# Sixteen tiny loads in the load queue of a retention and two-MLP kernel's prologue

## The chip, the cores and the metric

The kernel runs on one core of a Trainium2 chip, in one launch. The time is the device time of that core in microseconds, as the median of several runs. Beside the runs there is one profiled execution, from which all rows below come.

## What is computed

Retention over q, k and v (4 batches, 8 heads, 576 tokens, 64 dimensions), then two MLPs over the 2,304 tokens of 512 features, each with 2,048 hidden features, all in float32:

```
scores = (q @ k.T) / 8
D[i, j] = gamma[h] ** (i - j)  where i >= j, else 0;  gamma[h] = 1 - 2 ** (-5 - h)
x  = (scores * D) @ v                     # heads side by side: 2304 x 512
h  = max(x @ w_in, 0);  x = (h * h) @ w_out
h  = x @ w2_in;  y = (h * clip(h + 3, 0, 6) / 6) @ w2_out
```

## The kernel before

The tokens stand in 18 chunks of 128. The first MLP goes over five blocks of 512 or 384 tokens and, within a block, over 16 slices `f` of 128 hidden features: `h_part` (line 645) makes h of a slice, `a_part` (line 689) adds its part of the output to four accumulators. The retention of the first four chunks is done in a prologue (the functions named `first_...`), that of the others in between the slices of the first MLP (`retention`, `visit`). The second MLP follows with other tiles (lines 1243 and 1298).

Matrix products on TensorE take each float32 operand as two parts, a rounded one and its residue. The weights of the first MLP come as 64-bit words, so each half slice, a tile of 512 KB (128 rows of 4 KB), goes through four steps: `load_w` brings it (line 133; tile `raw_0_f_i`, half i of slice f: i = 0 is for h, i = 1 for the accumulation), `scale_w` scales its two halves on ScalarE (lines 143, 144), `narrow_w` joins them on VectorE (lines 161, 162), `cast_w` rounds on ScalarE (line 170) and `low_w` makes the residue on GpSimd or VectorE (line 177). The order of the instructions on each engine is the order in which the code is written.

The prologue's loads are all issued on SyncE, in one order, written out by hand. The tiles that they fill: `q_c` holds q and k of chunk c transposed (line 211, 512 KB), `kv_c` k and v by rows (line 217, 512 KB), `con0` and `con` three pieces of the constants (lines 887, 891, 904); `con` is the last of them, first read by `scale_k` of chunk 4 (line 419).

```python
    load_t(0)
    nc.sync.dma_start(con0[:, :QD0], cst[:, :QD0])
    load_kv(0)
    load_t(1)
    load_kv(1)
    nc.sync.dma_start(con0[:, QD0:], cst[:, QD0:DK0])
    load_t(2)
    load_kv(2)
    load_w(0, 0, (0,))
    load_t(3)
    load_kv(3)
    load_w(0, 1, (0,))
    ...
    load_w(0, 3, (1,))
    nc.sync.dma_start(con, cst[:, DK0:])
```

Behind them SyncE issues, for chunk 4, `k`, `q`, `v` and four pieces of `qs` (lines 225, 226, 233, 412), and then the weights from slice 4 on. Every load raises one of eight semaphores, DMAHW0 to DMAHW7, which are given to the loads in turn; before SyncE issues a load, it waits until the load that had the same semaphore before has landed, that is the one eight places ahead. SyncE goes through its instructions in order, so a load that waits holds up all behind it.

The compute part of the prologue ends with `h_part(0, 0, 0)`, whose tokens come in two halves; the second half needs `x` of chunk 3 (`first_x(3)`, line 338, on ScalarE). On ScalarE the order there is: cast w_0_0_0, scale raw_0_1_0, x of chunk 3, scale raw_0_0_1, cast w_0_1_0 (made from raw_0_1_0 and read by the second `h_part`), scale raw_0_2_0.

`align` is a tile of 128 x 80 float32 that only takes room: nothing reads or writes it.

Of the kernel before, what the change touches and what calls it, by code (L numbers as in the profile page):

```python
# [11 lines left out]
F32 = mybir.dt.float32  # L12
# [7 lines left out]
P = 128  # L20
# [69 lines left out]
def retention_moe_kernel(ctx: ExitStack, tc, qk, kv, w1, w2, cst, out):  # L90
# [5 lines left out]
    nc = tc.nc  # L96
# [3 lines left out]
    def pool(stack, name, bufs, **kw):  # L100
        return stack.enter_context(tc.tile_pool(name=name, bufs=bufs, reuse_waits="tile", **kw))

    left, right = ExitStack(), ExitStack()
# [4 lines left out]
    xapool = pool(left, "xapool", 1, side="left")  # L108
    whi = pool(left, "whi", 1, side="left")

    pool(ctx, "align", 1, side="right").tile([P, 80], F32, tag="align", name="align")
    upool = pool(ctx, "upool", 1, side="right")
    wlo = pool(right, "wlo", 1, side="right")
    xbpool = pool(right, "xbpool", 1, side="right")
# [13 lines left out]
    def load_w(ph, f, halves=(0, 1)):  # L128

        src = w1.bitcast(I32)  # L130
        for i in halves:
            t = (wlo if f < NJ else whi).tile([P, DM, 2], I32, tag=f"w{f}_{i}", name=f"raw_{ph}_{f}_{i}")
            nc.sync.dma_start(
                t, src[f, :, 2 * DM * i : 2 * DM * (i + 1)].rearrange("p (n t) -> p n t", t=2)
            )
            raws[ph, f, i] = t
# [68 lines left out]
    def load_t(c):  # L205
        if c:
            tag = (None, f"w{NF - 5}_0", f"w{NF - 2}_0", f"w{NF - 2}_1")[c]
            t = whi.tile([P, 2, NPAIR, P], F32, tag=tag, name=f"q_{c}")
        else:
            t = apool.tile([P, 2, NPAIR, P], F32, tag="q", name=f"q_{c}")  # L210
        nc.sync.dma_start(t, qk[c].rearrange("p x (n t) -> p x n t", n=NPAIR))
        ch[c] = [t[:, 0], t[:, 1]]

    def load_kv(c):
        tag = (f"w{NF - 6}_0", f"w{NF - 5}_1", f"w{NF - 3}_0", f"w{NF - 3}_1")[c]
        t = whi.tile([P, 2, DM], F32, tag=tag, name=f"kv_{c}")
        nc.sync.dma_start(t, kv[c])
        ch[c] += [t[:, 0], t[:, 1]]
# [506 lines left out]
    def new_x(ph, blk):  # L725
        nb, tag = BLOCKS[blk]
        p = xbpool if tag == "xb" else xapool
        xs[ph, blk] = p.tile([P, 2, NC, nb], F32R, tag=tag, name=f"x_{ph}_{blk}")
# [142 lines left out]
            fn(*a)  # L871


    nc.gpsimd.memset(nought, 0.0)

    def idle_matmuls(n):
# [17 lines left out]
    load_w(0, 0, (0,))  # L894
    load_t(3)
    load_kv(3)
    load_w(0, 1, (0,))
    load_w(0, 0, (1,))
    load_w(0, 2, (0,))
# [1 line left out]
    load_w(0, 3, (0,))  # L901
    load_w(0, 2, (1,))
    load_w(0, 3, (1,))
    nc.sync.dma_start(con, cst[:, DK0:])
    new_x(0, 0)

# [446 lines left out]
```

## Time and profile before

| | us |
|---|---|
| median of 3 runs | 801.71 |
| lowest and highest | 801.16, 802.65 |
| the profiled execution, its own time | 802.4 |
| its span, first to last instruction | 800.6 |
| TensorE busy | 794.1 |
| VectorE, ScalarE, GpSimd busy | 587.1, 400.9, 165.3 |

In the profile PE is TensorE's matmuls, PEld its weight loads, DVE VectorE, ACT ScalarE, POOL GpSimd, SP SyncE; L133 is line 133 of the kernel. Names of tiles have their numbers left out, so that raw stands for every raw_0_f_i. Times count from the first instruction. A load's time to landing runs from the start of its issue on SyncE until its last part is in place.

### The profile page before, as it was taken

How to read it: one execution, taken by the hardware profiler on the slowest of the kernel's cores; microseconds unless marked ns; L12 is line 12 of the kernel's file. 1: busy time of each engine (PE TensorE's matmuls, PEld its weight loads, DVE VectorE, ACT ScalarE, POOL GpSimd, SP SyncE). 2: the span in 40 equal slices, each digit the busy share in tenths (PEclk: the TensorE clock that was granted, in tenths of full speed). 3: DMA queues.
4: the chain of work that ended last, by engine and by line, in shares of the span. 5: the costliest groups of instructions: out<-in, count | busy, mean ns of one | idle time of the engine just before them, and what ended most of it. 6: DMA issues, size and time to landing. Idle time of an engine off the chain costs nothing.

```text
span 800.6 us, 16540 instructions
## 1 busy us (share of the span) xinstructions
PE 794.1 (99%) x6396; PEld 740.2 (92%) x6396; DVE 587.1 (73%) x1083; ACT 400.9 (50%) x746; POOL 165.3 (21%) x154
## 2 busy tenths in 40 slices
PE   8999999999999999999999999999999999999998
PEld 7878889999888899998888899999999999999998
DVE  4888987888755577775547876988577987677864
ACT  4797745444444444444445533666234655244553
POOL 4212230211001011100000065600255500256300
PEclk9999999999999999999999999999999999999999
DMA  9966627777746487856448887988887979877884
GB/s 340 344 222 222 221 93 221 221 221 229 217 139 199 123 249 222 224 159 191 138 141 263 246 303 253 321 294 292 276 260 247 355 255 305 277 242 260 272 278 142
DMA packets 148062, 189.66 MB, mean 237 GB/s; under 512 B 22416, under 2 KB 101904, under 8 KB 147984
## 3 DMA queue, kind: packets, MB, share of 16 engines
q1 hardware_dynamic: 147984, 188.61, 73.8%
q8 instruction: 50, 0.82, 0.4%
q14 instruction: 28, 0.23, 0.1%
HBM read 149.78 MB, written 38.80 MB: 236 GB/s over the span
## 4 chain that ended last, share of the span: by engine, by line
PE 95%; ACT 2%; DVE 1%; DMA 1%; issue 0%; POOL 0%; SPq 0%; DVEq 0%; ACTq 0%; POOLq 0%
PE acc L689 24%; PE h L645 23%; PE z L1243 22%; PE z L1298 21%; PE at L518 2%; DMA kv<-kv_dram 1%; PE alone L518 0%; PE o L282 0%; ACT w L170 0%; ACT raw L143 0%; ACT raw L144 0%; DVE wt L162 0%; PE sums L282 0%; PE sc L261 0%; DVE r L663 0%
## 5 line engine op out<-in xcount | busy, mean ns | idle before, releaser
L689 PE MATMUL acc<-g,w 128*128 128x512 f32 (+1 forms) x960 | 212.6, 370 | 0.0
L645 PE MATMUL h<-x,w 128*128 128x512 f32 (+2 forms) x972 | 211.1, 365 | 0.3 <-ACT w L170 0.3
L645 PEld LDWEIGHTS h<-x,w 128*128 128x128 f32 x972 | 175.8, 188 | 23.2 <-ACT w L170 0.7
L689 PEld LDWEIGHTS acc<-g,w 128*128 128x128 f32 x960 | 173.8, 188 | 23.7 <-DVE g L671 0.3
L1243 PE MATMUL z<-xop,ring 128*128 128x384 f32 x1008 | 175.3, 334 | 0.0
L1243 PEld LDWEIGHTS z<-xop,ring 128*128 128x128 f32 x1008 | 174.7, 188 | 0.1
L1298 PE MATMUL z<-ring,spl 128*128 128x256 f32 x1512 | 172.2, 276 | 0.0
L1298 PEld LDWEIGHTS z<-ring,spl 128*128 128x128 f32 x1512 | 172.1, 188 | 0.0
L1159 POOL TENSOR_TENSOR aop<-aop,aop 128x384 f32<-128x384 f32 x96 | 108.1, 1137 | 293.4 <-DVE aop L1156 289.6
L1181 DVE TENSOR_TENSOR spl<-aop,spl 128x384 fp32r<-128x384 f32 x168 | 98.5, 604 | 31.2 <-ACT spl L1177 29.2
L1177 ACT ACTIVATE spl<-aop 128x384 fp32r<-128x384 f32 x168 | 86.3, 523 | 54.5 <-PE z L1298 48.5
L660 ACT ACTIVATE r<-h 128x512 f32<-128x512 f32 (+1 forms) x79 | 43.7, 553 | 110.8 <-PE h L645 110.7
L1153 ACT ACTIVATE aop<-held,small 128x384 f32<-128x384 f32 x72 | 44.4, 617 | 108.4 <-DVE held L1119 107.9
L663 DVE TENSOR_TENSOR r<-r,h 128x512 f32<-128x512 f32 (+1 forms) x80 | 50.6, 632 | 52.2 <-ACT r L660 51.4
L1119 DVE TENSOR_TENSOR held<-z,held 128x384 f32<-128x384 f32 x120 | 66.5, 554 | 28.6 <-PE z L1243 26.5
L665 ACT ACTIVATE g<-r 128x512 fp32r<-128x512 f32 (+1 forms) x80 | 47.1, 589 | 64.2 <-DVE r L663 64.2
L671 DVE TENSOR_TENSOR g<-r,g 128x512 fp32r<-128x512 f32 (+1 forms) x80 | 53.8, 672 | 20.9 <-ACT g L665 18.5
L1156 DVE SCALAR_TENSOR_TENSOR aop<-aop,held 128x384 f32<-128x384 f32 x72 | 50.1, 696 | 17.8 <-ACT aop L1153 16.1
L415 POOL TENSOR_TENSOR qs<-qs,con 128x512 f32<-128x512 f32 x11 | 14.9, 1359 | 138.0 <-DMA qs<-qk_dram 125.7
L779 ACT ACTIVATE uhi<-seven 128x896 fp32r<-128x896 f32 x32 | 30.5, 955 | 24.1 <-DVE seven L769 13.7
L784 DVE TENSOR_TENSOR seven<-seven,uhi 128x896 fp32r<-128x896 f32 x32 | 34.9, 1091 | 7.8 <-ACT uhi L779 7.5
L177 POOL TENSOR_TENSOR w<-wt,w 128x512 fp32r<-128x512 f32 x14 | 19.0, 1357 | 69.2 <-ACT w L170 59.8
(114 smaller groups left out, 610.0 us busy)
## 6 DMA issues: line engine op xcount, KB each, us to landing
ring<-w_out_hl SPq DMA_DIRECT2D x84, 512.0 KB, 4.9
ring<-w_in_hl SPq DMA_DIRECT2D x72, 512.0 KB, 4.8
raw<-w_dram SPq DMA_DIRECT2D x32, 512.0 KB, 7.0
uraw<-w_dram SPq DMA_DIRECT2D x64, 256.0 KB, 3.3
q<-qk_dram SPq DMA_DIRECT2D x18, 512.0 KB, 5.4
w_in_hl<-uhi SPq DMA_DIRECT2D x16, 448.0 KB, 3.7
w_in_hl<-seven SPq DMA_DIRECT2D x16, 448.0 KB, 4.5
w_out_hl<-uhi SPq DMA_DIRECT2D x16, 448.0 KB, 3.3
```

Source lines behind the costliest of these rows:

```text
L645: nc.tensor.matmul(hp[:, ts], w[:, wi, c * P : (c + 1) * P], x[:, xi, c, ts], start=k == 0, stop=k == 3 * NC - 1,)
L663: nc.vector.tensor_tensor(r, r, hp[:, :nb], ALU.mult)
L665: nc.scalar.activation(g[:, 0, :nb], r, AF.Copy)
L671: nc.vector.tensor_tensor(g[:, 1, :nb], r, g[:, 0, :nb].bitcast(F32), ALU.subtract)
L689: nc.tensor.matmul(acc[d][:, :nb], wt, g[:, gi, :nb], start=first, stop=stop)
L1119: fn(*a)
L1156: stt(f32(q, j), f32(q, j), 6.0, h, ALU.min, ALU.mult)
L1159: nc.gpsimd.tensor_tensor(f32(o, j), f32(a, j), f32(b, j), op)
L1177: act(t[:, 0, :], f32(q, k), AF.Copy)
L1181: tt(t[:, 1, :], f32(q, k), t[:, 0, :].bitcast(F32), ALU.subtract)
L1243: nc.tensor.matmul(bank[q], w[:, wi, u * P : (u + 1) * P], x[:, u, xi, :], start=k == 0 and q not in (2, 4, 3), stop=k == 5, skip_group_ch ...
L1298: nc.tensor.matmul(o, sp[:, g, P * n : P * (n + 1)], w[:, k % 2, wi, :], start=k == 0 and m == 0 and n % 2 == 0 and q not in (2, 4, 3), st ...
```

## The change

The tile that only took room gets a name, and two sets of eight loads write into it: 2, 4, 6, 8, 10, 12, 14 and 15 rows of 5 to 12 numbers (20 to 48 bytes) of the table of constants, side by side. The first set stands behind the load of kv_3, the second ahead of the load of `con`. Nothing reads what they bring. Lines behind the new function move by 6 to 8.

```diff
-    pool(ctx, "align", 1, side="right").tile([P, 80], F32, tag="align", name="align")
+    spare = pool(ctx, "align", 1, side="right").tile([P, 80], F32, tag="align", name="align")
...
+    def small_loads():
+        at = 0
+        for i, n in enumerate((2, 4, 6, 8, 10, 12, 14, 15)):
+            nc.sync.dma_start(spare[:n, at : at + 5 + i], cst[:n, :5 + i])
+            at += 5 + i
+
...
     load_t(3)
     load_kv(3)
+    small_loads()
     load_w(0, 1, (0,))
...
     load_w(0, 2, (1,))
     load_w(0, 3, (1,))
+    small_loads()
     nc.sync.dma_start(con, cst[:, DK0:])
     new_x(0, 0)
```

The first place is on SyncE, at the load of kv_3, in the kernel before. In brackets stands the semaphore that the instruction waits for (the number behind its name has no meaning here); align is the spare tile, w1_dram the first MLP's weights.

```order
L211 DMA q_3_147<-qk_dram 128x1024 [waits DMAHW1_49]
L217 DMA kv_3_149<-kv_dram 128x1024 [waits DMAHW2_49]
L133 DMA raw_0_1_0_151<-w1_dram 128x1024 [waits DMAHW3_49]
L133 DMA raw_0_0_1_153<-w1_dram 128x1024 [waits DMAHW4_49]
L133 DMA raw_0_2_0_155<-w1_dram 128x1024 [waits DMAHW5_49]
L133 DMA raw_0_1_1_157<-w1_dram 128x1024 [waits DMAHW6_49]
```

The same place in the changed kernel:

```order
L217 DMA kv_3_149<-kv_dram 128x1024 [waits DMAHW2_49]
L877 DMA align_73<-cst_dram 2x5 [waits DMAHW3_49]
L877 DMA align_73<-cst_dram 4x6 [waits DMAHW4_49]
L877 DMA align_73<-cst_dram 6x7 [waits DMAHW5_49]
L877 DMA align_73<-cst_dram 8x8 [waits DMAHW6_49]
L877 DMA align_73<-cst_dram 10x9 [waits DMAHW7_49]
L877 DMA align_73<-cst_dram 12x10 [waits DMAHW0_49]
L877 DMA align_73<-cst_dram 14x11 [waits DMAHW1_49]
L877 DMA align_73<-cst_dram 15x12 [waits DMAHW2_49]
L133 DMA raw_0_1_0_159<-w1_dram 128x1024 [waits DMAHW3_49]
```

The eight new loads take each of the eight semaphores once; the last of them, align with 15 rows, has the semaphore of kv_3 and waits for kv_3 to land. Raw_0_1_0 stands behind it and waits for the first of the new loads, where it waited for q_1, which stood eight places ahead.

The second place is on SyncE, at the load of con, in the kernel before (k_4 is the next chunk's k):

```order
L133 DMA raw_0_2_1_161<-w1_dram 128x1024 [waits DMAHW0_49]
L133 DMA raw_0_3_1_163<-w1_dram 128x1024 [waits DMAHW1_49]
L904 DMA con_102<-cst_dram 128x1040 [waits DMAHW2_49]
L225 DMA k_4_400<-kv_dram 128x512 [waits DMAHW3_49]
```

and in the changed kernel:

```order
L133 DMA raw_0_3_1_171<-w1_dram 128x1024 [waits DMAHW1_49]
L877 DMA align_73<-cst_dram 2x5 [waits DMAHW2_49]
L877 DMA align_73<-cst_dram 4x6 [waits DMAHW3_49]
L877 DMA align_73<-cst_dram 6x7 [waits DMAHW4_49]
L877 DMA align_73<-cst_dram 8x8 [waits DMAHW5_49]
L877 DMA align_73<-cst_dram 10x9 [waits DMAHW6_49]
L877 DMA align_73<-cst_dram 12x10 [waits DMAHW7_49]
L877 DMA align_73<-cst_dram 14x11 [waits DMAHW0_49]
L877 DMA align_73<-cst_dram 15x12 [waits DMAHW1_49]
L912 DMA con_102<-cst_dram 128x1040 [waits DMAHW2_49]
L225 DMA k_4_416<-kv_dram 128x512 [waits DMAHW3_49]
```

Con keeps its semaphore, but the load eight places ahead of it is now a tiny one, and the tiny load just ahead of it waits for that of raw_0_3_1. On the other engines no instruction is added, taken away or moved.

## Rows read from the trace of the kernel before

**Rows 1.** The page's first part: busy us (share of span) x instructions.
```profile
PE 794.1 (99%) x6396; PEld 740.2 (92%) x6396; DVE 587.1 (73%) x1083; ACT 400.9 (50%) x746; POOL 165.3 (21%) x154
```

**Rows 2.** Busy time by stage; columns in the first line of the fence.
```profile
core 0: us, PE busy (x) PEld busy (x) DVE busy (x) ACT busy (x) POOL busy (x), PEclk, DMA share, GB/s
...
10.00:20.00 10.00, 9.29 (x166) 8.46 (x168) 7.31 (x12) 7.38 (x17) 6.95 (x7) 1.00 1.02 407
...
28.00:48.00 20.00, 20.00 (x131) 16.35 (x131) 17.90 (x32) 15.90 (x29) 1.30 (x1) 1.00 0.95 297
48.70:130.00 81.30, 81.30 (x805) 67.86 (x806) 69.96 (x124) 56.59 (x103) 18.52 (x15) 1.00 0.55 180
```

**Rows 3.** Timeline, SyncE's DMA issues, 5 to 48 us: start, duration, line, target, count.
```profile
6.31 0.44 SPq L211 DMA_DIRECT2D q<-qk_dram  x1
7.64 0.33 SPq L217 DMA_DIRECT2D kv<-kv_dram  x1
8.89 7.57 SPq L133 DMA_DIRECT2D raw<-w_dram  x7
18.53 0.33 SPq L904 DMA_DIRECT2D con<-cst_dram  x1
...
28.80 5.65 SPq L133 DMA_DIRECT2D raw<-w_dram  x6
```

**Rows 4.** DMA issues of 6.2 to 9 us: count, KB each, median us to landing.
```profile
q<-qk_dram SPq DMA_DIRECT2D x1, 512.0 KB, 9.8
kv<-kv_dram SPq DMA_DIRECT2D x1, 512.0 KB, 10.9
```

**Rows 5.** The same view, issues of 0.7 to 1.6 us.
```profile
q<-qk_dram SPq DMA_DIRECT2D x1, 512.0 KB, 3.5
```

**Rows 6.** The same view, issues of 18.5 to 24 us.
```profile
con<-cst_dram SPq DMA_DIRECT2D x1, 520.0 KB, 10.3
```

**Rows 7.** The same view, issues of 23.6 to 29 us.
```profile
raw<-w_dram SPq DMA_DIRECT2D x1, 512.0 KB, 6.9
qs<-qk_dram SPq DMA_DIRECT2D x4, 64.0 KB, 8.6
```

**Rows 8.** DMA queue 8 (packets, MB, share): whole span, 15.0 to 16.7, 21.75 to 22.9 us.
```profile
q8 instruction: 50, 0.82, 0.4%
...
q8 instruction: 1, 0.02, 3.7%
...
q8 instruction: 1, 0.02, 6.0%
```

**Rows 9.** Timeline of ScalarE, 19 to 48.5 us; in brackets idle time and releaser.
```profile
19.81 0.70 ACT L143 ACTIVATE raw<-raw 128x512 f32<-128x512 f32 x1
...
22.58 0.63 ACT L338 ACTIVATE x<-xf 128x512 fp32r<-128x512 f32 x1 [1.49 <-DVE xf L334]
23.12 0.68 ACT L143 ACTIVATE raw<-raw 128x512 f32<-128x512 f32 x1
...
24.27 0.61 ACT L170 ACTIVATE w<-wt 128x512 fp32r<-128x512 f32 x1
...
38.91 0.68 ACT L143 ACTIVATE raw<-raw 128x512 f32<-128x512 f32 x1
```

**Rows 10.** Timeline of VectorE, 21 to 48 us.
```profile
25.40 0.69 DVE L658 TENSOR_SCALAR r<-h 128x512 f32<-128x512 f32 x1
...
38.25 0.69 DVE L419 TENSOR_TENSOR k<-k,con 128x512 f32<-128x512 f32 x1
...
40.06 0.42 DVE L161 TENSOR_SCALAR wt<-raw 128x512 int32<-128x512 int32 x1
```

**Rows 11.** Timeline of TensorE, 17 to 52 us.
```profile
21.64 6.35 PE L645 MATMUL h<-x,w 128*128 128x256 f32 x36
27.82 2.89 PE L689 MATMUL acc<-g,w 128*128 128x512 f32 x12
...
48.70 3.02 PE L645 MATMUL h<-x,w 128*128 128x512 f32 x12 [0.27 <-ACT w L170]
```

## The prediction

> **What bounds the kernel now.** I read the page's first part, then busy time by stage, then the single loads of the first 40 us. TensorE is busy for 99% of the span [rows 1], so time is lost only where TensorE waits, and the table by stage says where that is [rows 2]: 0.7 us are missing between 10 and 20 us, nothing between 28 and 48 us, nothing from 48.7 to 130 us. A delay of TensorE at the start therefore has nothing later to vanish in: what is still there at 48.7 us is there at the end. In the same rows the DMA engines are full (share 1.02) from 10 to 20 us and 0.95 busy from 28 to 48 us; after 48.7 us they are half idle. So the question is what sixteen loads do to a full DMA queue in the first 40 us, and how much of it reaches TensorE before 48.7 us.
>
> SyncE's rows show how the queue is kept full [rows 3]. The order listing gives each load the semaphore that it waits for; there are eight, taken in turn, so load n goes out when load n-8 has landed. The fourth q went out at 6.31 and landed 9.8 us later, at 16.1; the fourth kv at 7.64, landing 10.9 us later, at 18.5 [rows 3, 4]. Con, eight behind kv, went out at 18.53, the moment kv landed. Raw_0_1_0 went out at 8.89 and ScalarE took it at 19.81 [rows 9]. A load lands some 10 us after its issue only because seven others are ahead of it. Alone, a load of 512 KB takes 3.5 us [rows 5].
>
> **The change, first set.** It moves no instruction of the compute engines; SyncE issues sixteen loads more. Their bytes are nothing (71 rows of 20 to 48 bytes a set), but each holds one of the eight semaphores until it lands, and the eight follow each other. The last waits for kv, 18.53 us. Only behind it comes raw_0_1_0, which went out at 8.89 [rows 3]. An issue takes 0.33 us, and 0.05 us lie between two: 18.9 us. By then the queue has run dry, so it lands after 3.5 us [rows 5], at 22.4, where it had landed at 19.8: **2.6 us later**. The six weight loads behind it go out in a row and land one per 1.29 us (512 KB at 407 GB/s [rows 2]): raw_0_0_1 at 23.7, the last at 30.1. It had landed at about 27.5, one load ahead of con (18.53 + 10.3 = 28.8 [rows 3, 6]).
>
> What does TensorE feel of it? ScalarE started to scale raw_0_1_0 at 19.81, right at its landing, took 1.15 us for both halves, then idled for 1.49 us until x at 22.58 [rows 9]. Now scaling starts at 22.45 and x at 23.6: the idle time absorbs 1.5 of 2.6 us, **1.05 us remain**. Behind x stand raw_0_0_1 (23.12, now 24.2; landed at 23.7, in time) and the cast of w_0_1_0 (24.27, now 25.3) [rows 9]. The second h needs that cast, and the 36 matmuls of the first two h ran from 21.64 to 27.8 with gaps, the accumulation following directly [rows 11]. So TensorE leaves this place 1.05 us late. VectorE follows less closely: its relu at 25.40 [rows 10] stands behind the joining of raw_0_0_1's two halves, 0.69 us like the relu, which can now end at 24.2 + 1.15 + 0.69 = 26.05: 0.7 us late, and with the residue of w behind ScalarE's cast 0.8. Since the one wait left in the loop, 0.27 us before 48.70 [rows 11], is at the end of the ScalarE chain and that of VectorE, 0.2 us can be won back there: 0.85 us.
>
> **An instruction fetch falls into it.** Queue 8 moved 50 packets of 0.82 MB in all [rows 8], 16 KB each; 50 x 256 is 12,800, and TensorE has 12,792 instructions with its weight loads [rows 1], so they are its own. One lies in 15.0 to 16.7 us, and kv landed 2.4 us behind q where 1.29 is the rate: 1.1 us lost on the engine that carried it. The next lies in 21.75 to 22.9 us [rows 8]. TensorE begins h at 21.64 in both kernels, so it stays there. Before, raw_0_0_1 had landed by then (19.8 + 1.29); now raw_0_1_0 or raw_0_0_1 is on the engines. Raw_0_0_1 at 23.7 + 1.1 = 24.8 would be 0.6 us late for ScalarE at 24.2, and the total 1.45 us. The Trainium skill (DMA: Bandwidth & Descriptors, Queues, rings and completion order) says that an engine alternates between its queue rows a whole packet at a time; the 1.1 us agree with a fetch of that size standing ahead of one load's share. Between 0.85 (it misses) and 1.45 (it hits) I take **1.3 us**, nearer the second, since the loads are in flight at that time.
>
> **Second set.** It empties the queue a second time: its last load waits for the last weight load, 30.1 us, or 31.2 with the fetch. Con goes out 0.4 us behind, lands 3.5 us later: 34.0 to 35.1 instead of 28.8. Its first reader is k at 38.25 [rows 10]: covered by over 3 us, as are k, q and v, which follow at the rate (up to 37.7). The first weight load behind them, raw_0_4_0, landed at 28.80 + 6.9 = 35.7 [rows 3, 7], 6.9 us behind con; by bytes alone (1,792 KB at the rate) it would be 4.4. I take 5.7, between them, because the four qs loads with short runs are in both: 39.7 to 40.8. ScalarE wants it at 38.91 [rows 9], now 40.2, and a further 0.46 us cost nothing, since VectorE reads the first half at 40.06 [rows 10] and that was done at 39.6: 40.7. So no term for the second set, but hardly any margin. Its cover is ScalarE's backlog; where raw_0_4_0 comes at the late end, 35.1 + 6.9 = 42.0, the kernel loses 1.3 us more.
>
> The issues themselves cost SyncE 16 x 0.33 = 5.3 us, in which nothing else could have gone out: counted above. Sixteen is twice eight, so all later loads keep their semaphores.
>
> **Sum.** 1.3 us, bounds 0.8 (the fetch misses and the whole 0.27 us are won back) and 2.6 (the late end of the second set). The profiled execution is 802.4 us (span 800.6) and would be 803.7; the median of the runs is 0.7 lower, 801.71, and gives **803.0 us**, 0.16% up. About 0.2%, 1.6 us, is what a measurement here can tell from no change.
>
> **Rivals.**
> - *Raw_0_4_0 comes last.* Everything as above, but the second refill is late for ScalarE at 40.7 us; from there each microsecond is one of the end. For it: con 35.1 with the fetch, and 6.9 us behind con in the trace. Against it: in the trace the engines were unevenly loaded by the first fetch, and after an idle queue they start even. At the late end 804.3 us, slower than can be missed. Chance 0.2.
> - *The refill is hidden.* If kv lands earlier because the queue behind it is empty (17.4 us, the 1.1 us of the first fetch gone), raw_0_1_0 lands at 21.3 and x keeps its 22.58: 801.7 to 802.1 us. Against it: the fetch lies at TensorE's own place, which the change doesn't touch. 0.1.
> - *Tiny loads are paid one after the other.* The four qs loads, 64 KB each, landed 8.6 us after their issue, in the stream of the others [rows 7]; were each tiny load to hold the queue for the 3.5 us of a load alone, eight would put raw_0_1_0 some 28 us back and the time above 825 us. The Trainium skill (DMA: Bandwidth & Descriptors, Rules for kernel authors) says that transfers under 64 KB are mostly overhead, and advises to coalesce them. By that rule such a price is to be expected; rows here show loads overlapping, seven deep. 0.04.
> - *The change doesn't do what it says*, or the emptier queue serves someone sooner: 801.0 or less; nothing in the rows waits for that. 0.05.
>
> **How the numbers follow.** The forecast case, 802.3 to 803.5, has 0.61. The range 801.6 to 804.6 takes in the bounds of the sum and the first two rivals. Slower by over 1.6 us, that is above 803.3: the first rival's 0.2, the third's 0.04, and a fifth of the forecast case, since 1.45 us and a little stall pass the line: 0.36. Faster: 0.04. The rest, 0.60, lies within.
>
> **What would show it.** In the changed profile raw_0_1_0's issue stands at 18.9, not 8.89, with some 3.5 us to its landing; ScalarE scales it at 22.4; h's accumulation starts about 29 us, not 27.82; con goes out at 30.5 to 31.6; the DMA share falls below 0.7 around 19 to 21 and 31 to 34 us; from 48.7 us on all rows of TensorE are shifted by one amount. I am wrong if raw_0_1_0 is issued before kv has landed, if ScalarE's x stays at 22.6, if the shift at 50 us is not that at the end, or if ScalarE waits for raw_0_4_0 for more than 0.5 us.

## The result, and the profile after

| | before | after |
|---|---|---|
| median of the runs, us | 801.71 | 806.52 |
| lowest and highest | 801.16, 802.65 | 806.37, 806.94 |
| the profiled execution, its own time | 802.4 | 806.37 |
| its span | 800.6 | 804.6 |

The changed kernel is slower: the ratio is 1.0059, 95% interval 1.0037 to 1.0082, some 4.7 us where 1.3 were forecast, and outside the range. TensorE's work has not grown: it is busy 1.4 us longer (794.1 before [rows 1]), and 2.6 us more are spent waiting. The page's first part of the changed kernel:

```profile
PE 795.5 (99%) x6396; PEld 740.6 (92%) x6396; DVE 588.6 (73%) x1083; ACT 400.9 (50%) x746; POOL 161.7 (20%) x154
```

By stage, to be read beside [rows 2] (columns in the first line of the fence):

```profile
core 0: us, PE busy (x) PEld busy (x) DVE busy (x) ACT busy (x) POOL busy (x), PEclk, DMA share, GB/s
10.00:20.00 10.00, 9.37 (x177) 8.54 (x173) 6.93 (x12) 6.30 (x14) 7.49 (x8) 1.00 0.62 233
20.00:28.00 8.00, 5.64 (x30) 5.05 (x30) 4.82 (x8) 5.20 (x10) 2.06 (x2) 0.81 0.98 313
28.00:52.00 24.00, 22.25 (x138) 17.63 (x138) 19.47 (x34) 17.17 (x32) 1.30 (x1) 0.99 0.90 314
52.00:134.00 82.00, 82.00 (x808) 68.06 (x807) 70.62 (x125) 57.13 (x105) 18.49 (x15) 1.00 0.56 190
```

TensorE loses 2.4 us between 20 and 28 us and 1.75 us between 28 and 52 us; from 52 us on it is as full as before. The DMA engines moved 233 GB/s between 10 and 20 us, where it had been 407.

SyncE's DMA issues of the changed kernel, as in [rows 3] (align is the spare tile of the tiny loads):

```profile
5.93 0.41 SPq L217 DMA_DIRECT2D kv<-kv_dram  x1
7.87 9.63 SPq L877 DMA_DIRECT2D align<-cst_dram  x8
17.55 4.37 SPq L133 DMA_DIRECT2D raw<-w_dram  x7
21.96 9.77 SPq L877 DMA_DIRECT2D align<-cst_dram  x8
31.78 0.39 SPq L912 DMA_DIRECT2D con<-cst_dram  x1
...
33.63 2.69 SPq L412 DMA_DIRECT2D qs<-qk_dram  x4
36.37 5.16 SPq L133 DMA_DIRECT2D raw<-w_dram  x6
```

The eighth tiny load goes out as kv_3 lands (17.16 us), raw_0_1_0 0.39 us behind: that wait is as the prediction has it. In this execution kv_3 landed 1.35 us earlier than in [rows 3, 4] (18.51). The emptier queue behind it is hardly the reason: in second_only and set_later, where weight loads follow kv_3 as before, it landed at 17.54 and 17.08 us, so it varies from run to run. The two profiles are off by it at the start.

ScalarE's timeline of the changed kernel, beside [rows 9]; idle time and releaser in brackets:

```profile
22.18 0.67 ACT L143 ACTIVATE raw<-raw 128x512 f32<-128x512 f32 x1 [4.01 <-DMA raw<-w_dram]
...
23.29 0.63 ACT L338 ACTIVATE x<-xf 128x512 fp32r<-128x512 f32 x1
...
26.31 0.70 ACT L143 ACTIVATE raw<-raw 128x512 f32<-128x512 f32 x1 [0.62 <-DMA raw<-w_dram]
...
43.31 0.67 ACT L143 ACTIVATE raw<-raw 128x512 f32<-128x512 f32 x1 [2.90 <-DMA raw<-w_dram]
```

Two places, one for each set: at 22.18 us it waits for raw_0_1_0, at 43.31 us for raw_0_4_0. TensorE's timeline shows what becomes of them, beside [rows 11]:

```profile
19.93 1.69 PE L645 MATMUL h<-x,w 128*128 128x256 f32 x12
23.98 6.03 PE L645 MATMUL h<-x,w 128*128 128x256 f32 x24 [2.36 <-ACT x L338]
29.85 2.89 PE L689 MATMUL acc<-g,w 128*128 128x512 f32 x12
...
46.69 3.01 PE L645 MATMUL h<-x,w 128*128 128x512 f32 x12 [1.75 <-ACT w L170]
49.54 3.11 PE L689 MATMUL acc<-g,w 128*128 128x512 f32 x12
52.64 3.00 PE L645 MATMUL h<-x,w 128*128 128x512 f32 x12
```

The accumulation starts at 29.85 instead of 27.82 (2.0 us late), the h that had its 0.27 us wait at 48.70 now starts at 52.64: 3.94 us late, and the span is 4.0 us longer. So all that is lost is lost before 52.6 us; what each set has to do with it, the experiments show. At the first place 24 matmuls took 6.03 us, and the windows' row for 20 to 28 us has a granted clock of 0.81: it was halved (1.2 instead of 2.4 GHz) from 24.91 to 28.32 us, after TensorE had waited 2.36 us.

When each of the seven weight loads behind the first set landed, by the trace's records of their completion:

```
              issue   landings, us                                          apart
before         8.89   19.79 21.05 22.34 23.61 24.89 26.16 27.45             1.3 each
after         17.55   22.16 23.90 26.29 27.58 28.86 30.18 31.40             1.74, 2.39, then 1.3
raw_0_4_0:  before 35.68 (8.2 behind the last of them), after 43.28 (11.9 behind it)
```

### The profile page after: what moved, and what is told of

Same layout as the page of the kernel before. It is cut to its first block, busy times and chain, and to the rows that moved or that the text cites. A ratio compares the mean times of both kernels' runs of the same rounds, so it can differ in the third digit from the quotient of the medians.

```text
span 804.6 us, 16556 instructions
## 1 busy us (share of the span) xinstructions
PE 795.5 (99%) x6396; PEld 740.6 (92%) x6396; DVE 588.6 (73%) x1083; ACT 400.9 (50%) x746; POOL 161.7 (20%) x154
## 4 chain that ended last, share of the span: by engine, by line
PE 95%; DMA 3%; ACT 1%; SPq 1%; issue 0%; DVE 0%
PE acc L689 24%; PE h L645 24%; PE z L1251 22%; PE z L1306 21%; PE at L518 2%; DMA kv<-kv_dram 2%; DMA raw<-w_dram 1%; PE alone L518 1%; SPq L412 0%; ACT raw L143 0%; PE sc L430 0%; PE o L481 0%; ACT raw L144 0%; PE sc L441 0%; PE o L491 0%
## 5 line engine op out<-in xcount | busy, mean ns | idle before, releaser
L1167 POOL TENSOR_TENSOR aop<-aop,aop 128x384 f32<-128x384 f32 x96 | 106.2, 1116 | 295.3 <-DVE aop L1164 291.5
L1189 DVE TENSOR_TENSOR spl<-aop,spl 128x384 fp32r<-128x384 f32 x168 | 100.5, 617 | 30.7 <-ACT spl L1185 28.7
L671 DVE TENSOR_TENSOR g<-r,g 128x512 fp32r<-128x512 f32 (+1 forms) x80 | 53.1, 664 | 20.9 <-ACT g L665 18.5
```

Of the source, the lines that this page charges most:

```text
L671: nc.vector.tensor_tensor(g[:, 1, :nb], r, g[:, 0, :nb].bitcast(F32), ALU.subtract)
L1167: nc.gpsimd.tensor_tensor(f32(o, j), f32(a, j), f32(b, j), op)
L1189: tt(t[:, 1, :], f32(q, k), t[:, 0, :].bitcast(F32), ALU.subtract)
```

## Experiments

Two theories stood against each other. **The drained queue**: a set costs nothing for what it brings, but its last load makes SyncE wait until the queue is empty, and what stands behind comes late by the time that the refill takes. **The transfers**: sixteen DMAs cost their own time wherever they stand. For the size of the loss a third cause was open, TensorE's **clock**. Edits are shown against the changed kernel. A ratio is always that to the kernel before, run on the same chip in the same session.

### One set at a time

first_only leaves out the second call of small_loads(), second_only the first:

```diff
     load_w(0, 3, (1,))
-    small_loads()
```

> Only the first set of eight, behind kv_3. Theory (the set empties the load queue; the refilled weights come late for ScalarE, TensorE waits for x of chunk 3 and then runs for some 3 us at half clock): the accumulation of slice 0 starts some 2 us later than in the kernel before, raw_0_4_0 is in time again, so 2.0 to 3.5 us are lost: 803.7 to 805.2 us. Rival (each set costs by itself, by its tiny transfers): half of the 4.8 us, 804.1 us, with no waiting of ScalarE for raw_0_1_0 longer than 1 us. Rival (the clock never matters): 1.0 to 1.5 us.

Measured: 804.67 us, ratio 1.0047 (1.0031 to 1.0063), the single runs between 803.07 and 807.96. It lies in the first theory's range, and the rival's 804.1 is near; the second set decides between them.

> Only the second set, ahead of con. Theory: the queue is emptied at 27.4 us instead of 31.4, so raw_0_4_0, which landed 11.9 us behind the last weight load in the changed kernel, lands at about 39.3, where ScalarE wants it at 38.9: 0 to 0.7 us lost, 801.7 to 802.4 us. The two sets together then cost more than the sum of each alone. Rival (each set costs by itself): half of 4.8 us, 804.1 us.

Measured: 801.92 us, 1.0008 (1.0000 to 1.0017). Raw_0_4_0 landed at 38.52 us, 12.1 us behind the last weight load, as late behind it as in the changed kernel; but the last weight load landed at 26.40 and ScalarE wanted raw_0_4_0 at about 38.9 [rows 9]. So alone the first set costs, the second next to nothing, and not the half that the rival gives it.

### The sets elsewhere

idle_place has both sets at 109 us, just ahead of a stretch in which SyncE issues next to nothing (in the kernel before nothing between 110.8 and 121.0 us); late_sets has them at 131 us, ahead of loads that are waited for (only the place differs: `if i == 14` behind retention(i), `if i == NF + 2` at the head of the loop):

```diff
+        if i == 14:
+            small_loads()
+            small_loads()
```

> Both sets issued about 109 us in, behind v of chunk 8, where SyncE has nothing to issue for some 12 us and nothing on the path waits for a load behind them; none in the prologue. Theory (a set costs what the loads behind it come late for their readers): within 0.5 us of before. Rival (the sixteen loads cost by themselves, in whatever place): 4 us or more, as in the changed kernel and with both sets at 131 us.

Measured: 801.32 us, 1.0000 (0.9991 to 1.0009).

> Both sets issued during the second block of tokens (some 135 us in), where the load queue is half idle; none in the prologue. Theory (only the emptied queue costs): within 0.5 us of before, 801.2 to 802.2 us. Rival (sixteen more loads cost something wherever they stand, 0.3 us each on SyncE or in the queue): 2 to 4.8 us.

Measured: 810.14 us, 1.0110 (1.0097 to 1.0123), more than the change itself. This expectation missed, since the place was not idle. SyncE's issues of late_sets, and below them the two waits of TensorE and what ran behind them:

```profile
131.12 8.03 SPq L877 DMA_DIRECT2D align<-cst_dram  x16
139.26 0.92 SPq L744 DMA_DIRECT2D uraw<-w_dram  x2
140.22 2.66 SPq L412 DMA_DIRECT2D qs<-qk_dram  x4
```

```profile
146.26 0.37 PE L518 MATMUL at<-qs,state 64*64 64x64 f32 x2 [4.09 <-POOL qs L415]
149.69 0.37 PE L518 MATMUL at<-v,k 64*64 64x64 f32 x2 [2.30 <-DMA v<-kv_dram]
...
150.75 4.21 PE L689 MATMUL acc<-g,w 128*128 128x384 f32 x12
154.76 2.70 PE L645 MATMUL h<-x,w 128*128 128x384 f32 x12
157.30 2.24 PE L689 MATMUL acc<-g,w 128*128 128x384 f32 x12
```

The qs loads went out at 140.22 instead of 135.01 us, and TensorE waited 6.4 us for what they and v bring. The clock was halved there for 10.2 us (145.49 to 155.74), in which twelve matmuls of an accumulation took 4.21 us and not 2.24, as the next twelve, and twelve of h 2.70 and not 2.25, as those ahead of the wait: 2.4 us more. Wait and clock together make the 8.8 us. The same sixteen loads cost nothing at 109 us and 8.8 us at 131 us: the price is that of the loads queued behind them, with what the clock adds. The Trainium skill (DMA: Bandwidth & Descriptors, Anatomy of one DMA) says that the DMA engines wait on no semaphore and that such a wait is held by the issuing sequencer; SyncE's rows agree: eight tiny loads, each issued in 0.25 to 0.32 us, take 9.63 us from the first to the last in the changed kernel. Its rule that transfers under 64 KB are mostly overhead (Rules for kernel authors), the prediction's third rival, is not seen in the time of the kernel: ratio 1.0000 for sixteen of them at 109 us.

### One load that waits for kv_3, four loads, and the set two places later

one_dependent has no set, but one copy of ten numbers of kv_3 itself, so that SyncE waits for kv_3 with a single transfer. first_four has four loads in the first set, so that raw_0_1_0 waits for kv_2 and three loads of 512 KB are still on their way. set_later has the first set behind raw_0_0_1. None has a second set.

```diff
     load_kv(3)
-    small_loads()
+    nc.sync.dma_start(spare[:2, :5], ch[3][2][:2, :5])
```

```diff
-        for i, n in enumerate((2, 4, 6, 8, 10, 12, 14, 15)):
+        for i, n in enumerate((2, 4, 6, 8)):
```

```diff
     load_kv(3)
-    small_loads()
     load_w(0, 1, (0,))
     load_w(0, 0, (1,))
+    small_loads()
     load_w(0, 2, (0,))
```

> In place of the first set one tiny copy, of 2 rows of 5 numbers of kv_3 into the spare tile, so that SyncE waits for kv_3 to land before it issues raw_0_1_0; no second set. Theory (the emptied queue costs, not the eight transfers): as with the first set alone, 803.5 to 806 us. Rival (eight loads of a few bytes cost by their own transfers or completions): at most 0.6 us above before, 802.0 us.

Measured: 804.00 us, 1.0033 (1.0022 to 1.0044): one transfer that empties the queue costs what eight do (1.0047, and 1.0024 in a later session). SyncE's issues of one_dependent:

```profile
16.91 0.73 SPq L903 DMA_DIRECT2D align<-kv  x1
17.69 3.80 SPq L133 DMA_DIRECT2D raw<-w_dram  x7
```

> First set alone and with four loads instead of eight; no second set. Raw_0_1_0 then waits for kv_2, not for kv_3, and goes out some 5 us earlier, with three loads of 512 KB still on their way. Theory (what costs is that the queue runs dry): raw_0_1_0 lands within 0.5 us of its 19.8, time within 0.2% of the kernel before. Rival (a thinner queue costs in proportion): half of what eight cost, 1.3 to 2 us, 802.7 to 803.5.

Measured: 801.43 us, 0.9992 (0.9984 to 1.0001): four transfers that leave it filled cost nothing that these runs tell. SyncE's issues of first_four, and below them the start of TensorE's h and accumulation, without a wait as in [rows 11]:

```profile
8.07 3.50 SPq L877 DMA_DIRECT2D align<-cst_dram  x4
12.57 7.19 SPq L133 DMA_DIRECT2D raw<-w_dram  x7
```

```profile
20.45 6.34 PE L645 MATMUL h<-x,w 128*128 128x256 f32 x36
26.63 2.91 PE L689 MATMUL acc<-g,w 128*128 128x512 f32 x12
```

> The first set two loads later, behind raw_0_0_1; no second set. Theory: raw_0_1_0 and raw_0_0_1 go out as in the kernel before, TensorE does not wait for x of chunk 3, raw_0_2_0 lands at about 25.5 where ScalarE wants it at 24.8; 0.5 to 1.5 us lost, 801.9 to 802.9 us, and the clock stays up. Rival (a set costs the same wherever it stands in the prologue): 804.7 us.

Measured: 802.19 us, 1.0004 (0.9995 to 1.0013). The queue drains here too (raw_0_2_0 went out at 20.07 and landed at 24.93 us, 4.9 us later), but ScalarE wants that load only then. What costs is a drain whose first load is wanted at once.

### TensorE's clock

The idle matmuls that the kernel already has for its start are put between the two halves of the first h, where TensorE waits: 16 in first_busy (first set only), 8 in first_busy8 (the same), 8 in both_busy (both sets).

```diff
         parts = 2 if ph == blk == f == 0 else 1
         for i in range(parts):
+            if i:
+                idle_matmuls(8)
```

> Only the first set, and 16 matmuls whose result nobody reads between the two halves of the first h, where TensorE waits for x of chunk 3. Theory: the granted clock stays at its upper level between 24 and 29 us, the 24 matmuls behind the wait take some 4.5 instead of 6.0 us, and the time is 1.0 to 1.7 us below that of the kernel with the first set alone. Rival (the slow matmuls wait for weights, not for the clock): the same time as with the first set alone, within 0.4 us.

Measured: 805.19 us, 1.0050 (1.0037 to 1.0062). The sixteen took 3.7 us, longer than the wait (2.36 us in the changed kernel), so this one says little.

> The changed kernel with 8 matmuls whose result nobody reads, between the two halves of the first h. Theory: the clock stays at its upper level, the accumulation of slice 0 starts about 1 us earlier than in the changed kernel; but raw_0_4_0 lands at the same time, some 43 us, because its landing hangs on the loads alone, so that ScalarE waits 1 us longer for it and the end is within 0.5 us of 806.5 us. Rival (the delays of the two sets add up): 1.0 to 1.6 us less than the changed kernel, 805.2 us.

Measured: 808.04 us, 1.0082 (1.0068 to 1.0096). Nothing was gained, as the theory has it, but the time is 1.5 us above its 806.5: both numbers were missed.

> First set alone, with 8 idle matmuls of TensorE between the halves of the first h (16 made TensorE late themselves). They take 1.95 us, less than TensorE waits there. Theory (in the first set's 3.3 us a part is TensorE's clock, halved after the wait): TensorE keeps its full clock, the second half of h and the second h take 4.4 us instead of up to 6.0, and the median falls below that of the first set alone (804.67) by 0.5 to 1.6 us, with a narrower spread. Rival (the clock falls in few runs of the first set alone, and the spread comes from the landing of kv_3): the median stays at 804.2 to 805.2.

Measured: 805.12 us, 1.0034 (1.0024 to 1.0045); with the first set alone it was 1.0047 and, in a later session, 1.0024. The rival's range, 804.2 to 805.2, was met: nothing gained that these intervals can tell. TensorE's timeline of both_busy:

```profile
25.28 4.42 PE L647 MATMUL h<-x,w 128*128 128x256 f32 x24
...
47.24 4.53 PE L647 MATMUL h<-x,w 128*128 128x512 f32 x12 [2.45 <-ACT w L170]
```

The clock now stays up at the first place (24 matmuls in 4.42 us, not 6.03), and nothing comes of it: TensorE waits longer at the second place, and there the clock was halved instead (47.10 to 50.52 us; 12 matmuls in 4.53 us instead of 3.0). Time won on TensorE at 25 us does not make raw_0_4_0 land sooner (43.82 us here). But a clock that falls at the second place costs: the next h started at 54.34 us, 10.5 us behind that landing, where it was 9.36 in the changed kernel (43.28 to 52.64).

### Raw_0_4_0 ahead of the qs loads

both_raw4_early keeps both sets and issues raw_0_4_0 right behind v, ahead of the four qs loads; both_raw4_busy8 adds the 8 idle matmuls.

```diff
     load_v(n0)
+    load_w(0, 4, (0,))
     load_qs(n0)
...
-                load_w(0, f + 4)
+                load_w(0, f + 4, (0, 1) if f else (1,))
```

> The changed kernel, with one move: raw_0_4_0, the first weight load behind the second set, is issued ahead of the four qs loads instead of behind them. Theory (the end is set by raw_0_4_0's landing, 43.28 us in the changed kernel, where ScalarE waits 2.90 us for it): the four qs loads landed 0.3 us apart at 39.3 to 40.2, so raw_0_4_0 lands 1.3 to 2.0 us earlier, the wait of ScalarE falls to about 1 us and the time by 1.3 to 1.9 us, to some 804.9. Rival (the second wait of TensorE comes from the clock that fell at 25 us and from the late cast, and raw_0_4_0 only hides behind it): no change, 806 to 807. Against both: qs is now late for POOL and TensorE: a new wait there, over 807.

Measured: 804.93 us, 1.0037 (1.0023 to 1.0051). Raw_0_4_0 landed at 42.00 us, 1.3 us earlier, and ScalarE's wait for it fell from 2.90 to 1.46 us.

> Both remedies together on the changed kernel: raw_0_4_0 ahead of qs, and 8 idle matmuls in the first wait. Theory (raw_0_4_0's landing set the end, which is why the idle matmuls alone gained nothing, 808.04): with raw_0_4_0 early they gain, 803.3 to 804.5, below raw_0_4_0 early alone. Rival (idle matmuls cost time wherever the wait is shorter than they last): above raw_0_4_0 early alone, 805 to 807.

Measured: 805.85 us, 1.0040 (1.0025 to 1.0055): no gain over the move alone. The median lies in the rival's range and above 804.93, but the two ratios, 1.0040 and 1.0037, can't be told apart, so the rival is not shown either.

These were compared across sessions, with intervals that overlap. So the changed kernel, the first set alone and the moved load ran again side by side:

> The changed kernel once more, beside the first set alone and beside the changed kernel with raw_0_4_0 early. Theory (the second set has a price of its own, through raw_0_4_0): ratio to the kernel before 1.005 to 1.008, above both others by 1.0 us or more. Rival (all of the loss is the first set's, and the difference was the session's): within 0.7 us of both others.

Measured: 807.76 us, 1.0071 (1.0057 to 1.0085).

> First set alone, in the same session as the changed kernel. Theory: 1.0 us or more below the changed kernel, ratio to the kernel before 1.003 to 1.005. Rival: within 0.7 us of it.

Measured: 803.99 us, 1.0024 (1.0015 to 1.0032).

> The changed kernel with raw_0_4_0 issued ahead of the four qs loads, in the same session. Theory (raw_0_4_0's landing sets the end): 1.3 us or more below the changed kernel, near the first set alone. Rival: within 0.7 us of the changed kernel.

Measured: 806.22 us, 1.0045 (1.0032 to 1.0057). The kernel before had 801.51 us there. So, side by side, the first set alone costs 1.9 us (0.0024 x 801.5; its ratio fell a little short of the forecast), both cost 5.7, and one load moved past four gives 2.1 us of it back by the ratios, 1.5 by the medians; 1.7 us above the first set alone remain, where the theory had it near. The second set, worth 0.6 us alone, is worth 3.8 us behind the first (2.5 to 5.1, an estimate from the two intervals). By the earlier ratios the same difference, 1.0059 less 1.0047, was 1.0 us: that it is more than the 0.6 is shown by these last runs only.

The profile of changed_again shows why, and without a drop of the clock (it is of the fastest of the five runs). Its chain of work that ended last, in order of time (start, duration, what), 6 to 56 us:

```profile
6.75 10.46 DMA kv<-kv_dram
17.22 0.32 SPq L877
...
21.70 10.32 DMA raw<-w_dram
32.04 0.32 SPq L877
...
32.41 0.39 SPq L912
...
36.34 0.62 SPq L412
...
37.00 6.42 DMA raw<-w_dram
...
43.44 0.67 ACT raw L143
...
46.25 0.53 ACT w L170
...
46.82 3.02 PE h L645 x12
49.85 2.89 PE acc L689 x12
...
52.76 3.06 PE h L645 x12
```

From 6.75 to 43.44 us no compute engine is on it: kv_3 lands and frees the last tiny load of the first set; seven weight loads follow, the last of which lands at 32.02; that frees the last tiny load of the second set; SyncE issues it, con, k, q, v and four qs, 4.96 us from 32.04 to 37.00, and raw_0_4_0 lands 6.4 us behind its own issue. Raw_0_4_0 at 43.28 (after) and 43.42 (here) puts the later h at 52.64 and 52.76, 9.35 us behind it; in three_ahead below it landed at 42.52 and that h started at 51.88, 9.36 behind. Counted back by 9.35 us from 48.70, raw_0_4_0 could have landed at 39.35 in the kernel before without harm (an estimate; it did at 35.68), and what it comes later than that, the h comes later. With second_only (38.52) it is in time.

### Why the refill is slow at first

three_ahead adds, to the first set alone, five tiny loads of four rows behind the third weight load, so that only three weight loads go out in a row after the drain and the others one by one:

```diff
     load_w(0, 2, (0,))
+    for i in range(5):
+        nc.sync.dma_start(spare[:4, 68 + 2 * i : 70 + 2 * i], cst[:4, :2])
```

> First set alone, and five more tiny loads behind the third weight load, so that after the drain three weight loads go out in a row (raw_0_1_0, raw_0_0_1, raw_0_2_0) and each of the other four only when one has landed. Theory (loads are slowed while SyncE issues seven of 512 KB 0.47 us apart): raw_0_0_1 and raw_0_2_0 land 1.3 to 1.5 us apart, and the time is 0.3 to 1 us below the first set alone. Rival (the engines are slow for some us behind a drain whatever is issued): 1.7 to 2.4 us apart as with the first set alone, time the same or above, since three loads of 512 KB may not fill the queue.

Measured: 804.82 us, 1.0035 (1.0023 to 1.0046). Raw_0_0_1 came 1.7 us behind raw_0_1_0 and raw_0_2_0 1.4 us behind that, nearer to the first theory, but raw_0_1_0 itself took 4.9 us, and the fifth and sixth load came 2.6 and 3.0 us behind the ones ahead of them, with the queue short again. The time did not fall. Both theories missed a part; the cause stays open.

## Why the prediction was wrong

**The mechanism was right, the refill was mis-sized.** Raw_0_1_0 was to be issued 0.4 us behind kv_3's landing and was (0.39). It was to land 3.5 us later, as a load alone [rows 5], and took 4.6; the next two were to follow at 1.29 us and came 1.74 and 2.39 us apart. In the other profiles with a drained queue the first load took between 3.7 and 5.0 us. So the last weight load stood 13.85 us behind the first one's issue, not 11.2: 2.65 us more. The Trainium skill (DMA: Bandwidth & Descriptors, Anatomy of one DMA) fits a DMA issued from GpSimd, not from SyncE as here, with some 2 us beside the bytes, by which 512 KB would be 3.2 us, an estimate; this case's 3.5 us is near it, its 3.7 to 5.0 us behind a drain lie above it.

I misread [rows 5]: that load was not alone but the first of seven issued from 0.74 to 3.56 us, as raw_0_1_0 is the first of seven, and the rows behind it showed a slow start. The third of them, issued at 1.65 us (in the kernel before):

```profile
kv<-kv_dram SPq DMA_DIRECT2D x1, 512.0 KB, 6.0
```

It landed at 7.62 us, 3.1 us behind the one ahead of it (a piece of the constants, at 4.48); in the changed kernel's profile the same load landed at 5.92.

**The second step that failed is "no term for the second set".** Raw_0_4_0 was put 9.6 us behind the last weight load (0.4 for con's issue, 3.5 to con's landing, 5.7 more); it came 11.9 us behind in after, 12.1 in second_only. Con's 3.5 us were nearly right (3.72); the 5.7 behind con, a mean of 4.4 by bytes (1,792 KB at 407 GB/s are 4.5) and 6.9 by the trace, measured 7.8. Con's landing, from which I counted, bound nothing: at 35.50 us it was done 0.87 us before raw_0_4_0 was issued. The better sum was in the rows: nine issues pass before its own (the last tiny load, con, k, q, v, four qs), 4.6 us by the single issues of the kernel before (an estimate: 0.33 us each, 0.60 to 0.72 for a piece of qs, 0.05 between two), and that load took 6.9 us from issue to landing [rows 7]; in after it was 4.97 and 6.92. With the prediction's own last weight load at 30.1 us that gives 41.6, beyond its limit of 40.7. The two mis-sized steps and the early kv_3 together give the landing: 39.7 + 2.65 + 2.3 - 1.35 = 43.3 us.

**The rival "raw_0_4_0 comes last" is what happened**, at 0.2 against 0.61: place and condition as told, but 2.6 us beyond the limit of 40.7 instead of 1.3. Its argument against itself, that the engines start even after an idle queue, did not help. **The rival "the refill is hidden"** had its condition, kv_3 at 17.16 us where it asked for 17.4, and failed all the same: raw_0_1_0 landed at 22.16, not 21.3.

**The two delays do not add up by the place at TensorE.** The path from kv_3 to raw_0_4_0 runs through the queue alone and has no slack; it overtakes whatever TensorE lost before, which is why the idle matmuls gave nothing. The prediction allowed for that, since its limit holds the 1.3 us already lost: 1.3 + (43.28 - 40.7) is 3.9. The landing was wrong, not this step.

**The instruction fetch** was not at 22 us in after: it lay at 17.33, while the queue was empty, as TensorE began h at 19.93 and not 21.64. Queue 8 of the changed kernel, 17.0 to 18.4 us (packets, MB, share):

```profile
q8 instruction: 1, 0.02, 4.0%
```

That term, 0.6 us of the sum, did not occur there; where it falls moves with the start of a run.

**TensorE's clock** had no term. It was halved for 3.4 us at the first place in after, not at all in the profile of changed_again, and both lost 4 us by 52.7: there it is no cause of its own. It is not cleared for the other runs. The profiled run of changed_again took 806.47 us at a mean clock of 1.000; the other four, at 0.997 or 0.998, took 806.96 to 809.28, and in both_busy a drop at the second place cost some 1.2 us (10.5 less 9.36, an estimate). How much of the median is the clock's stays open, and so does the share of the first set alone, since its two profiles are of runs below the median (803.07 us against 804.67, 803.49 against 803.99).

**What came as told**: the tiny loads are free in themselves, nothing changes behind 52 us, the shift at 52.6 is that at the end, con and its readers are covered. The sign by which I would be wrong, a wait for raw_0_4_0 of over 0.5 us, is the row at 43.31.

## What to carry to other kernels

A load that waits for a recent one, by its data or by the semaphore that it shares, drains the queue for all behind it, whatever its size; count what the refill costs from the moment that the queue is empty, as the issues that pass before the wanted load, one by one, and then its full time to landing in a filled queue. Several drains in a row make a chain through the queue that owes nothing to the compute engines: follow it to its end and compare with the time at which the last load is wanted, before looking at what each drain does at its own place. If such loads must stand somewhere, four that leave three large ones in flight, or a place where nothing is queued behind, cost nothing that could be measured here.

## What the runs showed that I had not expected

- A refilled queue is slow beyond its first load: 4 KB parts that take 159 ns each in the steady stream took up to 0.9 us in the first microseconds behind the drain in after, and the second and third load came mostly 1.5 to 2.4 us behind the one ahead of them. In the same way the kernel's own first loads (before) moved 268 to 364 KB per us between 3 and 8 us, where 400 is usual. Why stays open.
- The start of a run varies: TensorE's first h began between 19.8 and 22.5 us in the profiles of this case. The times spread too: first_four ran within 801.15 to 802.84 us, first_only within 803.07 to 807.96 and, later, 802.28 to 805.49, but the kernel before, over all sessions, within 800.77 to 804.31. That the drained queue turns the one into the other is not shown.
- Place counts for more than number: sixteen tiny loads were worth 0.0, 4.7 to 5.7, or 8.8 us.
